# Order of queued ScalarE and VectorE work in an attention + two-layer MoE-style kernel

## The chip, the cores and the metric

The kernel runs on one core of one Trainium2 chip, as one launch. The metric is the device time of one execution in microseconds (us); the median of several runs is compared. One execution is also profiled, which gives the instruction trace of every engine: TensorE (PE, with its weight loads PEld), VectorE (DVE), ScalarE (ACT), GpSimd (POOL) and the DMA queues, of which SP issues most.

## What is computed

```
# q, k, v: [2, 8, 768, 64]; centroids: [8, 16, 64]; all float32
q_assign = argmax(normalize(q) @ normalize(centroids).T)      # 16 clusters a head
k_assign = argmax(normalize(k) @ normalize(centroids).T)
scores   = where(q_assign == k_assign, q @ k.T / 8, -1e9)
attn     = softmax(scores) @ v                                # -> x: [1536, 512]

# first layer, w_in [512, 2048], w_out [2048, 512] (float64 in memory)
x = softplus(x @ w_in) @ w_out
# second layer, w_gate, w_val [512, 1536], w_out2 [1536, 512] (float64 in memory)
out = (silu(x @ w_gate) * (x @ w_val)) @ w_out2               # [1536, 512]
```

## The kernel before, in words

Every float32 operand of the two layers is held as a high and a low part of TensorE's reduced format, and a product is three matmuls: high x high, high x low, low x high. `w_split` makes the two parts of a weight: a ScalarE cast (`whi`, line 151) and a subtraction (`wlo`, line 152), which by then is VectorE's. Ahead of it, weights stored in 64 bits are narrowed to 32 in steps: *first* (ScalarE, line 124, reads the freshly loaded `raw`), *second* (VectorE, lines 126 and 129), *third* (VectorE, lines 133 and 137; it also issues the next weight loads on the SP queue). `two_tasks` makes five tasks for two weights: first, second, third, split, split. `pair_tasks` makes nine: first, second, third, two tasks of sums, and four splits.

The order of work on each engine is the order in which the program issues it; nothing is reordered later. So every step below is also a place in a queue, and an instruction that waits holds all that stand behind it on its engine. Lists of tasks are handed to the places between products (`run(between[i])`), or popped from `todo` a few at a time (`pump2`).

The first layer has 16 blocks of 128 hidden columns. Blocks 0 to 5 are computed plainly. Blocks 6 to 15 go in pairs (p = 3 to 7), each by seven products instead of eight, with sums of quarters of x and of the weights: `block_a(p)` does three of them, `block_b(p)` four. A product (`prod`, line 1087) is 12 matmuls of 384 columns into a bank pair of PSUM. In `block_a` the first product goes to x, ScalarE copies it to `p1` (line 1110), the second goes to y, and the third adds onto x, so it has to wait for that copy. The softplus of the last quarter of the pair before (line 1155) reads the x of that pair. Casts and subtractions of the hidden values (`g_high`, line 919; `g_low`, line 923) give the second matrix its operands. What `block_b` returns is a list `late`, which `block_a` of the next pair runs in two parts.

`y_group(g)` is the second product of pair g, and stands between the blocks of later pairs: six pieces j, 12 matmuls of 512 columns each (line 1002), over bank pairs O, W, X, Y. Pieces 0 to 2 (near) are added by VectorE to an accumulator on the chip (line 1020). Pieces 3 to 5 (far) are copied by ScalarE to a side buffer (line 1023), two of which alternate by j, and a GpSimd DMA adds them to `far_acc` in DRAM (line 1028). After the last `y_group` three SP loads (line 1209) bring `far_acc` back. `y_last` is the second product of the last pair: VectorE adds each half piece to the accumulator (line 1040), ScalarE casts it to YH (line 1041), and GpSimd or VectorE makes YL (line 1047).

The second layer begins with `plain_unit(0)`: its matmuls (line 854) take six of the banks that `y_last` has just used, the third of them the first half of bank pair Y, used by piece 3 of `y_last`. `one_` and `two_` are the tasks of the gate and value weights of units 0 and 1. Units 2 to 11 are `s_unit(f)`: seven products each, with `more()` between them, which runs the tasks in `todo`, and `fill(n)`, output pieces (line 1328) whose copy to a side buffer is line 1341. `a_half` casts and subtracts the hidden values of a unit.

Of the kernel before, what the change touches and what calls it, by code (L numbers as in the profile page):

```python
# [15 lines left out]
AF = mybir.ActivationFunctionType  # L16
# [18 lines left out]
def _h(ap, n=2):  # L35

    return ap.rearrange("p (a n) -> p a n", a=n)
# [3 lines left out]
def kernel(  # L41
# [123 lines left out]
    NPL = 3  # L165
# [736 lines left out]
    def run(tasks):  # L902
        for task in tasks:
            task()
# [13 lines left out]
    def g_high(f, e, cols):  # L918
        nc.scalar.copy(g_t[f][0][:, cols], e[:, cols])  # L919

    def g_low(f, e, cols):
        gh, gl = (x[:, cols] for x in g_t[f])
        nc.vector.tensor_tensor(out=gl, in0=e[:, cols], in1=_r(gh), op=ALU.subtract)
# [87 lines left out]
    def y_group(g, tags, order, between, bk0=None):  # L1011
        near = accs[0].rearrange("p a n -> p (a n)")
        for i, j in enumerate(order):
            bk = y_piece(g, j, tags[i], None if i else bk0)
            if j < 3:
                a = _h(near[:, 1024 * j:1024 * j + 1024])
                if g == 0:
                    nc.scalar.copy(a, bk)
                else:
                    nc.vector.tensor_tensor(out=a, in0=bk, in1=a, op=ALU.add)  # L1020
            else:
                st = _h(side[j % 2][:, 0:1024])
                nc.scalar.copy(st, bk)  # L1023
                a = _h(far_acc[:, 1024 * (j - 3):1024 * (j - 3) + 1024])
                if g == 0:
                    nc.sync.dma_start(out=a, in_=st)
                else:
                    nc.gpsimd.dma_start(out=a, in_=st, accum_op=ALU.add)  # L1028
            run(between[i])
# [71 lines left out]

    T0, T1 = slice(0, HT), slice(HT, NTOK)
    now = {}

    def block_a(p, between, late=()):
        g1 = S_t[("in", p), "1"]
        x = px("OX"[p % 2], "x")[:, :, 0:HT // 2]
        prod(x, g1, 0, qx(0, 0), True)
        p1 = p1_p.tile([128, 2, HT // 2], F32, tag="p1", name="p1")
        nc.scalar.copy(p1, x)  # L1110
        run(late[:1])
        y = px("Y", "y")[:, :, 0:HT // 2]
        prod(y, g1, 2, qx(1, 0), True)
        ev = tp.tile([128, NTOK], F32, tag="e", name="ev")
        nc.vector.tensor_tensor(out=_h(ev[:, T0]), in0=y, in1=p1, op=ALU.add)
        nc.scalar.activation(out=ev[:, T0], in_=ev[:, T0], func=AF.Softplus)
        run(late[1:])
        run(between[0])
        g3 = S_t[("in", p), "3"]
        prod(x, g3, 2, tqx(2))  # L1120
        eg = tp.tile([128, NTOK], F32, tag="e", name="eg")
        nc.scalar.copy(_h(eg[:, T0]), x)
        run(between[1])
        now[p] = g3, x, ev, eg

    def block_b(p, between):
        g3, x, ev, eg = now.pop(p)
        g2, g4 = (S_t[("in", p), n] for n in "24")
        fg, fv = 2 * p, 2 * p + 1

        def soft(src, e, cols, f):
            nc.scalar.activation(out=e, in_=src, func=AF.Softplus)

        w = px("W", "w")[:, :, 0:HT // 2]
        prod(w, g2, 0, tqx(3), True)
        nc.scalar.copy(_h(eg[:, T1]), w)
        g_home(fv)
        g_high(fv, ev, T0)
        g_low(fv, ev, T0)
        run(between[0])  # L1140
        prod(x, g3, 0, tqx(1))
        nc.vector.tensor_tensor(out=_h(eg[:, T1]), in0=x, in1=_h(eg[:, T1]), op=ALU.add)
        nc.scalar.activation(out=eg[:, T1], in_=eg[:, T1], func=AF.Softplus)
        g_home(fg)
        g_high(fg, eg, T1)
        run(between[1])
        prod(w, g4, 0, tqx(4))
        nc.vector.tensor_tensor(out=_h(eg[:, T0]), in0=w, in1=_h(eg[:, T0]), op=ALU.add)
        g_low(fg, eg, T1)
        nc.scalar.activation(out=eg[:, T0], in_=eg[:, T0], func=AF.Softplus)  # L1150
        g_high(fg, eg, T0)
        run(between[2])
        prod(x, g2, 2, qx(1, 1))
        g_low(fg, eg, T0)
        nc.scalar.activation(out=_h(ev[:, T1]), in_=x, func=AF.Softplus)
        run(between[3])
        return [lambda: g_high(fv, ev, T1), lambda: g_low(fv, ev, T1)]

    def three(*tags):
        tiles = [px(tag, "bank") for tag in tags]  # L1160
# [28 lines left out]
    pair, outs = in_pair_tasks(NPL + 1), out_tasks(NPL)  # L1189
    block_a(NPL, (tx3[2:3], tx3[3:]), [soft5])  # L1190
    y_group(2, "OWYOWY", MIX, (pair[0:1], pair[1:2], pair[2:3], pair[3:5], pair[5:7] + outs[0:1], outs[1:2] + pair[7:8]))
    late = block_b(NPL, ([], outs[2:3], outs[3:4], [])) + outs[4:5] + pair[8:9]
    for p in range(NPL + 1, NPAIRS - 1):
        pair, outs = in_pair_tasks(p + 1), out_tasks(p)
        block_a(p, (pair[0:1], pair[1:2]), late)
        y_group(p - 1, ("OX"[p % 2 - 1] + "WY") * 2, MIX, (pair[2:3], pair[3:5], pair[5:7], [pair[7], outs[0]], outs[1:2], outs[2:3]))
        late = block_b(p, (outs[3:4], outs[4:5], [], [])) + pair[8:9]
    outs = out_tasks(NPAIRS - 1)
    one_, two_ = (two_tasks([("gate", f), ("val", f)], "ac") for f in range(2))
    block_a(NPAIRS - 1, (outs[0:1], outs[1:2]), late)  # L1200
    run(block_b(NPAIRS - 1, ([], outs[2:3], outs[3:4], outs[4:5] + one_[0:1])))
    nc.scalar.activation(out=p1_p.tile([128, 1], F32, tag="x3", name="early"), in_=id32[:, 0:1], func=AF.Silu)
    y_group(NPAIRS - 2, "OYWXOY", (3, 4, 5, 0, 1, 2), (
        one_[1:2], one_[2:3], one_[3:4], one_[4:5] + two_[0:1], two_[1:2], two_[2:3]
    ))
    accs.append(mp.tile([128, 2, NTOK], F32, tag="t4", name="acc"))
    back = accs[1].rearrange("p a n -> p (a n)")
# [12 lines left out]

    YH = keep.tile([128, KD, NTOK], F32R, tag="xh", name="YH")
    YL = keep.tile([128, KD, NTOK], F32R, tag="xl", name="YL")
    y_last(NPAIRS - 1, "WXOYWX", ([], two_[3:4], two_[4:5], [functools.partial(t_sum, 0)], [], []))


    outv = out.rearrange("(b p t) d -> b p t d", b=B, t=NT)
# [19 lines left out]
    def pump2(steps):  # L1246

        for _ in range(-(-len(todo) // steps)):
            todo.popleft()()
# [94 lines left out]
        else:  # L1344
            nc.gpsimd.dma_start(out=out_of(n), in_=st, accum_op=ALU.add)  # L1345

    def s_unit(f):
        g1, g2, g3, g4 = (S_t[f, n] for n in "1234")
        last = f == NF2 - 1

        def quarter(k, t):
            return lambda part, kk: (YH, YL)[part][:, 2 * k + kk, HT * t:HT * t + HT]

        def tq(n):
            return lambda part, kk: T_t[n][part][:, HT * kk:HT * kk + HT]

        def fill(n):
            if f < 2 or last:
                return
            g, h = divmod(f - 2, 2)  # L1360
            o_out(g, 3 * h + n)

        left = [9]

        def more():
            pump2(left[0])
            left[0] -= 1

        t1, t2 = 0, 1
        sg_all = tp.tile([128, NTOK], F32, tag="e", name="sg")  # L1370
        sg = sg_all.rearrange("p (t c n) -> p t c n", t=2, c=2)
        x = px("X", "x")[:, :, 0:HT // 2]
        prod(x, g1, 0, quarter(0, 0), True)
        p1 = p1_p.tile([128, 2, HT // 2], F32, tag="p1", name="p1")
        nc.scalar.copy(p1, x)
        more()
        w = px("W", "w")[:, :, 0:HT // 2]
        prod(w, g2, 0, tq(3), True)
        nc.scalar.copy(sg[:, t2], w)
        more()  # L1380
        prod(x, g3, 2, tq(2))
        nc.scalar.copy(sg[:, t1], x)
        more()
        prod(w, g4, 0, tq(4))
        nc.vector.tensor_tensor(out=sg[:, t1], in0=w, in1=sg[:, t1], op=ALU.add)
        nc.scalar.activation(out=sg[:, t1], in_=sg[:, t1], func=AF.Silu)
        more()
        fill(0)
        more()
        prod(x, g3, 0, tq(1))  # L1390
        nc.vector.tensor_tensor(out=sg[:, t2], in0=x, in1=sg[:, t2], op=ALU.add)
        nc.scalar.activation(out=sg[:, t2], in_=sg[:, t2], func=AF.Silu)
        more()
        y = px("Y", "y")[:, :, 0:HT // 2]
        prod(y, g1, 2, quarter(1, 0), True)
        nc.vector.tensor_tensor(out=p1, in0=y, in1=p1, op=ALU.add)
        a_t[f] = pieces_of(f)
        nc.vector.tensor_tensor(out=sg[:, t1], in0=p1, in1=sg[:, t1], op=ALU.mult)
        more()
        fill(1)  # L1400
        more()
        prod(x, g2, 2, quarter(1, 1))
        nc.vector.tensor_tensor(out=sg[:, t2], in0=x, in1=sg[:, t2], op=ALU.mult)
        more()
        fill(2)
        a_half(f, sg_all, 0)
        a_half(f, sg_all, 1)
# [2 lines left out]
    rest = plain_unit(0)  # L1410
    todo.extend(rest)
    todo.extend(pair_tasks(NPLAIN, ("gate", NPLAIN), ("val", NPLAIN), "4321"))
    todo.extend(two_tasks([("out2", f) for f in range(NPLAIN)], "bb"))
    rest = plain_unit(1)
    while todo:
        todo.popleft()()
    todo.extend(rest)
    for f in range(NPLAIN, NF2):
        if f + 1 < NF2:
            todo.extend(pair_tasks(f + 1, ("gate", f + 1), ("val", f + 1), "4321"))  # L1420
        todo.extend(split_tasks(last_of(f)))
        s_unit(f)
    assert not todo

    G = NF2 // 2 - 2
# [51 lines left out]
```

## Time and profile before

| | |
|---|---|
| median of 3 runs | 804.28 us (803.09 to 804.67) |
| the profiled execution | 803.32 us |
| its span, first to last instruction | 801.5 us |
| mean granted TensorE clock | 0.992 of full speed |
| TensorE busy | 784.1 us, 98% |
| VectorE busy | 631.9 us, 79% |
| ScalarE busy | 495.1 us, 62% |
| GpSimd busy | 180.4 us, 23% |
| bytes moved by DMA | 104.17 MB, mean 130 GB/s |

A busy share of TensorE is no measure of its speed: matmuls are pipelined and their ends are modelled, so what counts is how far apart they start. The other engines' shares are those of instructions that really ran. Times in the views are counted from the first instruction.

### The profile page before, as it was taken

What the parts mean: (1) busy time and instruction counts of PE and PEld (TensorE: products, weight loads), DVE (VectorE), ACT (ScalarE), POOL (GpSimd) and SP (SyncE); (2) the same over time, 40 slices, a digit from 0 to 9 for tenths busy, and PEclk for the clock granted to TensorE, in tenths of its full rate; (3) what the DMA queues carried; (4) which work ended last, traced back from release to release, by engine and by line L of the source; (5) the groups of instructions that cost most, each with busy time, mean ns of one, the idle gap of its engine ahead of it and who ended that gap; (6) DMA issues with size and microseconds to landing.
All of it is one profiled execution on the core that took longest, in us unless ns stands there. A gap on an engine that the chain in (4) does not pass through costs nothing.

```text
span 801.5 us, 12250 instructions
## 1 busy us (share of the span) xinstructions
PE 784.1 (98%) x4545; PEld 712.5 (89%) x4545; DVE 631.9 (79%) x1012; ACT 495.1 (62%) x895; POOL 180.4 (23%) x178
## 2 busy tenths in 40 slices
PE   8999999999999999999999999899999999999997
PEld 7898899999998888889889898688899999999996
DVE  5988978989898888888677765899777777777763
ACT  5888889889897474546456365355654555555520
POOL 5635655556432000100100101400000101011100
PEclk8999999999999999999999999999999999999999
DMA  7875865765512322734835626403445676767554
GB/s 185 222 176 128 195 159 130 182 150 141 132 31 51 105 105 79 184 75 110 183 79 106 127 69 159 145 0 106 158 158 106 134 155 136 154 120 145 85 178 158
DMA packets 72796, 104.17 MB, mean 130 GB/s; under 512 B 29760, under 2 KB 52384, under 8 KB 72736
## 3 DMA queue, kind: packets, MB, share of 16 engines
q1 hardware_dynamic: 65552, 82.54, 35.5%
q0 software_dynamic: 5616, 20.45, 16.7%
q8 instruction: 36, 0.59, 0.3%
q10 hardware_dynamic: 1568, 0.39, 0.2%
q14 instruction: 24, 0.20, 0.1%
HBM read 52.99 MB, written 28.36 MB: 101 GB/s over the span
## 4 chain that ended last, share of the span: by engine, by line
PE 79%; DVE 9%; ACT 6%; DMA 3%; issue 2%; POOL 0%; ACTq 0%; DVEq 0%; SPq 0%; POOLq 0%
PE ob L1002 12%; PE x L1087 12%; PE ob L1328 11%; PE bank L854 8%; PE ops L596 8%; PE tps L579 7%; PE sps L547 7%; PE w L1087 6%; PE y L1087 3%; DMA raw<-in_moe_w_val_dram 2%; PE mps L421 2%; PE sims L458 1%; DVE wlo L152 1%; DVE m L133 1%; ACT gh L919 1%
## 5 line engine op out<-in xcount | busy, mean ns | idle before, releaser
L586 DVE TENSOR_TENSOR tl<-tps,th 128x384 fp32r<-128x384 f32 x192 | 98.8, 551 | 14.7 <-ACT th L585 14.4
L555 DVE TENSOR_REDUCE nm<-sps 128x1 f32<-128x768 f32 x96 | 91.3, 952 | 13.6 <-PE sps L547 10.3
L585 ACT CAST th<-tps 128x384 fp32r<-128x384 f32 x192 | 84.9, 492 | 16.8 <-PE tps L579 13.9
L579 PE MATMUL tps<-id,p 128*128 128x128 f32 x576 | 93.4, 279 | 1.7 <-DVE tl L586 1.7
L563 ACT ACTIVATE p<-sps,nm 128x768 f32<-128x768 f32 x96 | 88.2, 919 | 1.6 <-DVE nm L555 1.5
L547 PE MATMUL sps<-KT,QT 128*128 128x384 f32 x384 | 83.3, 338 | 1.3 <-ACT p L563 1.3
L579 PEld LDWEIGHTS tps<-id,p 128*128 128x128 f32 x576 | 75.0, 150 | 9.0 <-DVE tl L586 5.1
L596 PE MATMUL ops<-th,VV 128*128 128x256 f32 x288 | 80.0, 307 | 0.0
L596 PE MATMUL ops<-tl,VV 128*128 128x256 f32 x288 | 72.6, 282 | 0.0
L152 DVE TENSOR_TENSOR wlo<-m,whi 128x512 fp32r<-128x512 f32 (+1 forms) x66 | 41.6, 640 | 39.1 <-ACT whi L151 38.7
L1345 POOL DMA_DIRECT2D out_dram<-side x21 | 18.1, 864 | 219.2 <-ACT side L1341 219.2
L1028 POOL DMA_DIRECT2D far_acc<-side x18 | 15.7, 872 | 225.9 <-ACT side L1023 225.9
L151 ACT CAST whi<-m 128x512 fp32r<-128x512 f32 (+1 forms) x62 | 34.3, 565 | 50.2 <-DVE m L137 50.2
L547 PEld LDWEIGHTS sps<-KT,QT 128*128 128x128 f32 x384 | 63.4, 189 | 1.9 <-ACT p L563 1.7
L1328 PE MATMUL ob<-whi,aa 128*128 128x512 f32 x168 | 56.8, 392 | 0.0
L596 PEld LDWEIGHTS ops<-tl,VV 128*128 128x128 f32 x288 | 54.7, 190 | 0.1
L596 PEld LDWEIGHTS ops<-th,VV 128*128 128x128 f32 x288 | 54.4, 189 | 0.2
L1002 PE MATMUL ob<-gh,whi 128*128 128x512 f32 x168 | 51.8, 389 | 0.0
L1002 PE MATMUL ob<-gh,wlo 128*128 128x512 f32 x168 | 51.8, 389 | 0.0
L1002 PE MATMUL ob<-gl,whi 128*128 128x512 f32 x168 | 51.8, 389 | 0.0
L124 ACT ACTIVATE m<-raw 128x512 f32<-128x512 f32 x68 | 43.5, 669 | 9.8 <-DVE wlo L152 6.7
L1023 ACT COPY side<-ob 128x1024 f32<-128x1024 f32 x21 | 21.2, 1015 | 42.9 <-PE ob L1002 37.8
(254 smaller groups left out, 1995.7 us busy)
## 6 DMA issues: line engine op xcount, KB each, us to landing
raw<-in_moe_w_out_dram SPq DMA_DIRECT2D x28, 512.0 KB, 4.2
out_dram<-side POOLq DMA_DIRECT2D x21, 512.0 KB, 5.6
far_acc<-side POOLq DMA_DIRECT2D x18, 512.0 KB, 6.2
raw<-in_moe_w_in_dram SPq DMA_DIRECT2D x16, 512.0 KB, 6.1
raw<-in_moe_w_gate_dram SPq DMA_DIRECT2D x12, 512.0 KB, 3.6
raw<-in_moe_w_val_dram SPq DMA_DIRECT2D x12, 512.0 KB, 4.2
QT<-hi SPq DMA_DIRECT2D x30, 192.0 KB, 3.1
KT<-hi SPq DMA_DIRECT2D x14, 384.0 KB, 5.7
```

The lines of the kernel that those rows point to most:

```text
L152: low_on[0].tensor_tensor(out=lo, in0=x, in1=_r(hi), op=ALU.subtract)
L547: nc.tensor.matmul(ps[:, c, 0:384], lhsT=Q[:, a, 128 * j:128 * j + 128], rhs=K[:, a, 384 * c:384 * c + 384], start=(a == 0), stop=(a == 1),)
L555: nc.vector.tensor_reduce(out=nm, in_=ps[:, :, 0:384], axis=AX.XY, op=ALU.max, negate=True)
L563: nc.scalar.activation(out=_h(p), in_=s_t.pop(i)[:, :, 0:384], func=AF.Exp, bias=nm_t.pop(i), accum_out=sm_t[pr][:, j:j + 1],)
L579: nc.tensor.transpose(ps[:, 128 * j:128 * j + 128], p[:, 128 * kb:128 * kb + 128], id32)
L585: nc.scalar.copy(th, pv)
L586: nc.vector.tensor_tensor(out=tl, in0=pv, in1=_r(th), op=ALU.subtract)
L596: nc.tensor.matmul(o[:, 0:CW], lhsT=VV_t[pr][:, hh, kb].rearrange("p a d -> p (a d)"), rhs=t[:, kb, :], start=(kb == 0 and lohi == 0), sto ...
L854: nc.tensor.matmul(banks[c], lhsT=wt[:, kk, :], rhs=xt[:, kk, 512 * c:512 * c + 512], start=(kk == 0 and wt is hi and xt is xh), stop=(kk ...
L1002: nc.tensor.matmul(bk[:, t, :], lhsT=wt[:, 0, 128 * d:128 * d + 128], rhs=gt[:, 512 * c:512 * c + 512], start=(ff == 0 and n == 0), stop=( ...
L1087: nc.tensor.matmul(dst[:, c, :], lhsT=wt[:, at + kk, :], rhs=x(part, kk)[:, HT // 2 * c:HT // 2 * c + HT // 2], start=(first and kk == 0 a ...
L1328: nc.tensor.matmul(bk[:, t, :], lhsT=lhs[:, ts_], rhs=rhs[:, 0, :], start=(ff == 0 and i == 0), stop=(ff == 1 and i == 2),)
```

## The change

Four things move, and nothing is computed differently.

1. In `block_b` the last cast, softplus and subtraction of the gate half are not issued in place but returned in `late`, now five entries: cast of the gate half, last softplus, cast of the value half, and the two subtractions. `block_a` runs four entries of the list right after the copy of line 1110, and the rest after its softplus. The last split of the next pair's weights (`pair[8:9]`) moves from `late` to the fourth place of `block_b`.
2. In the last `y_group` the pieces run near and far in turns, 3, 1, 4, 2, 5, 0 instead of 3, 4, 5, 0, 1, 2.
3. The weight splits of unit 0 move one place earlier, together with the third step; the tasks of unit 1 move one place earlier each, and its two splits go from `y_last` to the last place of that `y_group`.
4. Of the tasks for the second layer's first two output weights, the third step now follows the evictions of unit 1, and the two splits stand in the second `more()` of `s_unit(2)`; unit 1's `a_half` casts all stand in its first `more()`.

```diff
+    LATE = 4
     def block_a(p, between, late=()):
...
         nc.scalar.copy(p1, x)
-        run(late[:1])
+        run(late[:LATE])
...
         nc.scalar.activation(out=ev[:, T0], in_=ev[:, T0], func=AF.Softplus)
-        run(late[1:])
+        run(late[LATE:])
...
         nc.scalar.activation(out=eg[:, T0], in_=eg[:, T0], func=AF.Softplus)
-        g_high(fg, eg, T0)
         run(between[2])
         prod(x, g2, 2, qx(1, 1))
-        g_low(fg, eg, T0)
-        nc.scalar.activation(out=_h(ev[:, T1]), in_=x, func=AF.Softplus)
         run(between[3])
-        return [lambda: g_high(fv, ev, T1), lambda: g_low(fv, ev, T1)]
+        def last_soft():
+            nc.scalar.activation(out=_h(ev[:, T1]), in_=x, func=AF.Softplus)
+        return [
+            lambda: g_high(fg, eg, T0), last_soft, lambda: g_high(fv, ev, T1),
+            lambda: g_low(fg, eg, T0), lambda: g_low(fv, ev, T1),
+        ]
...
-    late = block_b(NPL, ([], outs[2:3], outs[3:4], [])) + outs[4:5] + pair[8:9]
+    late = block_b(NPL, ([], outs[2:3], outs[3:4], pair[8:9])) + outs[4:5]
...
-        late = block_b(p, (outs[3:4], outs[4:5], [], [])) + pair[8:9]
+        late = block_b(p, (outs[3:4], outs[4:5], [], pair[8:9]))
...
-    y_group(NPAIRS - 2, "OYWXOY", (3, 4, 5, 0, 1, 2), (
-        one_[1:2], one_[2:3], one_[3:4], one_[4:5] + two_[0:1], two_[1:2], two_[2:3]
+    y_group(NPAIRS - 2, "OYWXOY", MIX[1:] + MIX[:1], (
+        one_[1:2], one_[2:5], two_[0:1], two_[1:2], two_[2:3], two_[3:5]
     ))
...
-    y_last(NPAIRS - 1, "WXOYWX", ([], two_[3:4], two_[4:5], [functools.partial(t_sum, 0)], [], []))
+    y_last(NPAIRS - 1, "WXOYWX", ([], [], [], [functools.partial(t_sum, 0)], [], []))
...
-    def s_unit(f):
+    def s_unit(f, lead):
...
         def more():
-            pump2(left[0])
+            if lead:
+                run(lead.pop(0))
+            else:
+                pump2(left[0])
             left[0] -= 1
...
-    todo.extend(two_tasks([("out2", f) for f in range(NPLAIN)], "bb"))
+    outs = two_tasks([("out2", f) for f in range(NPLAIN)], "bb")
+    todo.extend(outs[:2])
     rest = plain_unit(1)
     while todo:
         todo.popleft()()
-    todo.extend(rest)
+    run(outs[2:3])
     for f in range(NPLAIN, NF2):
...
-        s_unit(f)
+        s_unit(f, [rest, outs[3:]] if f == NPLAIN else [])
```

## Rows read from the trace of the kernel before

**Rows 1.** The page, busy time of each engine: TensorE's line.

```profile
PE 784.1 (98%) x4545; PEld 712.5 (89%) x4545; DVE 631.9 (79%) x1012; ACT 495.1 (62%) x895; POOL 180.4 (23%) x178
```

**Rows 2.** Waits of TensorE, 300 us to the end: total, times, longest.

```profile
PE bank L854 <- ACT YH L1041: 3.0, 1, 3.0
PE x L1087 <- ACT p L1110: 1.4, 3, 0.5
PE x L1087 <- ACT p L1375: 0.6, 1, 0.6
```

**Rows 3.** Timeline of TensorE into pair 7: start, us, what.

```profile
467.67 0.51 PE L1087 MATMUL y<-XH,wlo 128*128 128x384 f32 x2
468.66 0.98 PE L1087 MATMUL x<-Tx,whi 128*128 128x384 f32 x4 [0.49 <-ACT p L1110]
...
471.04 0.62 PE L1087 MATMUL w<-XH,whi 128*128 128x384 f32 x2
...
473.29 0.85 PE L1087 MATMUL x<-Tx,whi 128*128 128x384 f32 x4
```

**Rows 4.** Timeline of ScalarE and VectorE in the same stretch.

```profile
465.50 0.85 ACT L1150 ACTIVATE eg<-eg 128x768 f32<-128x768 f32 x1 [1.63 <-DVE eg L1148]
...
467.82 0.79 ACT L1110 COPY p<-x 128x768 f32<-128x768 f32 x1
...
468.64 0.96 DVE L1115 TENSOR_TENSOR ev<-y,p 128x768 f32<-128x768 f32 x1 [0.44 <-ACT p L1110]
...
469.63 0.85 ACT L1116 ACTIVATE ev<-ev 128x768 f32<-128x768 f32 x1 [0.29 <-DVE ev L1115]
...
470.38 0.60 ACT L151 CAST whi<-side 128x512 fp32r<-128x512 f32 x1
...
470.89 1.24 ACT L124 ACTIVATE m<-raw 128x512 f32<-128x512 f32 x2
...
472.03 0.80 ACT L1122 COPY eg<-x 128x768 f32<-128x768 f32 x1
```

**Rows 5.** The chain that ended last, 330 to 560 us: start, us, what.

```profile
370.80 2.08 PE y L1087 x12
...
372.90 2.36 PE x L1087 x12
375.26 16.36 PE ob L1002 x72
...
490.49 9.23 DMA raw<-in_moe_w_val_dram
```

**Rows 6.** Timeline of all engines at the turn of the layers.

```profile
504.86 1.28 DVE L1040 TENSOR_TENSOR acc<-ob,acc 128x512 f32<-128x512 f32 x2
...
512.22 0.64 PE L854 MATMUL bank<-YH,whi 128*128 128x512 f32 x2
...
513.10 1.39 DVE L152 TENSOR_TENSOR wlo<-m,whi 128x512 fp32r<-128x512 f32 x1 [1.21 <-ACT whi L151]
514.42 1.28 DVE L1040 TENSOR_TENSOR acc<-ob,acc 128x512 f32<-128x512 f32 x2
...
515.84 0.47 PE L854 MATMUL bank<-YH,whi 128*128 128x512 f32 x1 [2.99 <-ACT YH L1041]
```

**Rows 7.** Windows: busy time (count) by engine, clock, DMA share, GB/s.

```profile
516.00:520.00 4.00, 4.00 (x11) 3.12 (x11) 3.93 (x5) 1.57 (x4) 3.39 (x2) 0.57 0.01 4
```

**Rows 8.** DMA queues, 491 to 495 us (q0 GpSimd, q1 SP): packets, MB, share.

```profile
q0 software_dynamic: 171, 0.63, 99.8%
q1 hardware_dynamic: 12, 0.01, 1.5%
```

**Rows 9.** Tile `raw`, 470 to 520 us: time of its loads to landing.

```profile
DMA to landing us min/median/max: 4.4/8.4/12.5
```

**Rows 10.** Tile `acc`, 480 to 530 us: reload issues (ns, first and last start), landing.

```profile
L1209 SPq DMA_DIRECT2D acc<-far_acc x3: 382/423/567, 505.4 to 506.3; - x3
...
DMA to landing us min/median/max: 6.9/7.2/7.6
```

## The prediction, as written before the changed kernel was run

> **What bounds the kernel now.** I read the page first: TensorE is busy nearly the whole span [rows 1], so only the places where it stands still can pay. The view of waits, TensorE alone, from the first layer's weights to the end, names three such places [rows 2]: one wait of 3.0 us for a bank in the second layer's first unit (line 854), three of about 0.5 us for the copy of line 1110, and one of 0.6 us for line 1375. The timeline of each place then says how much later than due the next matmul began. The profile models a matmul's end, so starts are compared.
>
> At a pair boundary [rows 3], twelve matmuls of one product take 2.08 us [rows 5], so two take 0.35. The last two of y began at 467.67 and x was due at 468.02; it began at 468.66. Its first four then took 0.98 instead of 0.85. The boundary costs 0.64 + 0.13 = 0.77 us. The reader is to see why in ScalarE's queue [rows 4]: line 1110 empties the bank that x adds to, and starts at 467.82 because line 919 and the softplus of line 1155 stand ahead of it in the queue, though its input had been complete since y began, at 468.02 - 2.08 = 465.9.
>
> At the turn of the layers [rows 6], the first unit's third matmul was due at 512.22 + 2 x 0.23 = 512.68 and began at 515.84: 3.16 us. It wanted a bank that VectorE empties with the two additions (line 1040) at 514.42. Ahead of these stands a weight subtraction (line 152) at 513.10, which waited for its cast and took 1.39 us, where two additions of that width take 1.28. (A piece's matmuls follow each other by 16.36 / 72 = 0.227 [rows 5].) After the wait the granted clock was 0.57 on average over 4 us [rows 7] (1.2 GHz is 0.50, 2.4 GHz is 1.00): 4 x 0.43 = 1.7 us more.
>
> **The change, part by part.**
>
> *Bank copy first.* At the boundaries into pairs 5 and 6 ScalarE's order becomes: softplus 1150, the cast of the pair's last split (from the fourth place of block_b), copy 1110, then cast, softplus, cast. From [rows 4], which are those into pair 7 but stand for all: 1150 at 465.50, the cast 0.75 later (as 470.38 follows 469.63), the copy 0.51 later (as 470.89 follows 470.38) at 466.76, done at 467.55. That is before 468.02, so both waits go: 2 x 0.77 = 1.54. Into pair 4 there is little to win: y 2.08, x 2.36 [rows 5], so 0.28.
>
> Into pair 7, block_b follows at once, and ScalarE's work is only permuted. Copy 466.76, cast of the gate half about 467.5 to 468.3 (0.8, as line 1110 over as many elements), VectorE's subtraction of that half now ahead of line 1115, each 0.96 as that line's row has it, so softplus 1116 at about 470.2 (469.63 before); then two line-124 conversions and copy 1122 at 470.2 + 0.75 + 1.14 = 472.1, done 472.9. The x product of block_b reads behind that copy: 472.95 instead of 473.29 [rows 3], less a start of 0.13: 0.2 us, although the waits ahead of it vanish: 0.77, and 0.28 where w, due at 468.66 + 0.13 + 2.08 = 470.87, began at 471.04 and started as slowly (0.11). Queued behind the delayed 1116 are those conversions and VectorE's work on them; nothing on TensorE wants them for a product or more. The first term is 0.28 + 1.54 + 0.2 = **2.0 us**; ends 0 (the wait comes back at another bank, below) and 2.9 (pair 7 loses nothing).
>
> What this costs: softplus 1155 now frees its bank after the copy, about 467.55 + 0.7 + 0.85 = 469.1. The next y_group's first piece wants that bank at 468.02 + 2.08 = 470.1. Cover 1.0 us, hence nothing; a later copy costs its excess once per pair.
>
> *Splits out of y_last.* The two casts and two subtractions for unit 1 leave the eviction chain. A piece has 12 matmuls, 16.36 / 6 = 2.73 us [rows 5]; counted back from 512.22, pieces 0 to 5 of y_last are due at 495.9, 498.6, 501.3, 504.0, 506.8 and 509.5. Piece 3 ends at 506.8, so its additions need no longer wait for a split. The term is 3.16 + 1.7 = **4.9 us** if the bank is free by 512.7.
>
> *Where they go.* They now stand ahead of y_last, which makes VectorE's first eviction later, counted from the landing L of the last value weights. Before, L was 490.49 + 9.23 = 499.7 [rows 5] and the first eviction 504.86 [rows 6], 5.1 later. Two subtractions of 0.7 make it L + 6.5, and the bank for piece 4 free at L + 7.8. It is due at 506.8: no wait while L is under 499.0, beyond that one us for each. The evictions then run on: ten of 0.65 us to the bank in question, at L + 13 at the latest, in time while L is under 499.7.
>
> Why L should move: near and far pieces in turns put one accumulating transfer, not two, ahead of it. From 491 to 495, with the load issued at 490.49, the SP queue moved 12 packets, 0.01 MB of its 512 KB, while GpSimd's queue held the engines for 99.8% of the time [rows 8] with the transfers of two far pieces. One near addition now precedes the third step, so the load is issued about 1.3 later, near 491.8 (two additions, [rows 6]); with the shortest landing of 4.4 [rows 9], L is 496.2 as an estimate, with the longest of 12.5 it is 504.3. I take 496.2, since the second far transfer then follows the load.
>
> A rule speaks against this. The Trainium skill (DMA: Bandwidth & Descriptors, Queues, rings and completion order) says that each DMA engine takes turns between its queues, packet by packet. By that rule a queue's order would not bring L forward, and the sum would hold the second rival's 0.7 us wait. The rows disagree: 12 packets of this queue beside 171 of the other are no turns.
>
> *The same step's other queues.* The third step of unit 1 issues two weight loads on SP, now a piece earlier; the three reloads of the far accumulator stand behind them on SP and move too: from 505.4 [rows 10], 5.7 after L and with a near addition between, to about L + 4.4 = 500.6. They took 6.9 to 7.6 us to land, so near 508. Far piece 4's copy stands behind the casts of unit 0, which wait for VectorE: the second cast ends near 493.0, the copy with at most 1.3 at 494.3; its bank is due at 495.9, cover 1.6. Far piece 5's copy stands behind the conversion that waits for L: L + 0.6 + 1.3 = 498.1, its bank is due at 501.3, cover 3.2. Each costs its excess if the cover goes.
>
> *The second layer's start.* The out-weight casts move behind the evictions of unit 1. Four operations of 0.7 us lie between the second more() and fill(0), beside two products (4.2 us): nothing, or their excess. The wait of 0.6 at line 1375 (about 0.9 with the slow start) is VectorE's backlog. The same VectorE work stays ahead of it, in another order, so it may vanish (+0.9) or grow as much (-0.6, one row's size). No row settles it; evictions that come before splits favour a gain, and I take **0.3**.
>
> Sum: 2.0 + 4.9 + 0.3 = 7.2 us. The profiled execution took 803.32 us (its span 801.5 and 1.8 around it), which makes 796.1; the median of the runs is 0.96 above it, so against 804.28 the forecast is **797.1**. From the likeliest case's ends: with all of pair 7 and of line 1375 (0.9 + 0.6 more) gives 795.6; with line 1375 grown and only 1.1 at the boundaries, 798.9.
>
> **The rivals.**
>
> *The reload holds the bank.* The additions of piece 3 are the first that read the reloaded half. If the reload waits for the last far piece, now fifth instead of third, it is issued no earlier than before. Before, it landed about 505.4 + 7.2 = 512.6; then 1.28 for two additions, and the matmul at 514.0: 1.3 of the 4.9 stays. 798.4. For it: only the wait behind the split hid this. Against it: each reload reads one far piece, and the first two are early.
>
> *L stays.* At 499.7 piece 4 waits 0.7: 797.8. For it: two queues share the engines at any order. Against it, [rows 8]. (The Trainium skill's rule above would give this one.)
>
> *The boundaries give nothing.* The softplus behind the copy holds the next bank by what the copy won: 799.1. Against it, the cover of 1.0.
>
> *No change.* L at its slow end, 504.3: piece 4 waits 5.3, and a wait that long brings the clock down again (1.7), so 7.2 - 7.0 = 0.2: 804.1.
>
> *Slower.* The same conversion of line 124, now ahead of far piece 5's copy and of every eviction, waits past 504.5. From there 7.8 after L, and the clock, cost more than 7.2. At L = 508 it is 9.0 + 1.7 - 7.2 = 3.5 over: 807.8. For it: a load of this weight took 12.5 [rows 9]. Against it: that one stood behind two far pieces.
>
> **How the numbers follow.** A measurement of this kernel can tell about 0.2% (1.6 us) from no change. Chances: likeliest 0.56, reload 0.14, L stays 0.08, boundaries nothing 0.07, no change 0.08, slower 0.07. Faster takes the first four, less a hundredth: 0.84; same 0.09; slower 0.07. The range leaves out the last two and the edge above 798.9 that no rival gives: 795.0 to 800.8, the low end half a us under the best case, the high one at the boundaries' rival with line 1375 grown and L late.
>
> **What would show it.** After: line 1110 ends before y does at pairs 5 and 6, and no wait for it is left; x of block_b still follows line 1122 at pair 7. No line 152 between the evictions of y_last; the first unit's third matmul follows the second at once, and the clock stays at 1.00. Line 124 for the last value weights starts near 496. If the bank still waits with the evictions idle before a reload, the reload is the cause; if y_last's piece 4 waits, L is. A new wait at y_group's first piece would undo the boundaries.

## Result, and the profile after

The changed kernel takes 797.03 us (median of 4 runs, 796.30 to 798.76), the kernel before, timed beside it, 804.47 us (4 runs, 803.09 to 804.76). The ratio is 0.9914 with a 95% interval of 0.9894 to 0.9934: 7.4 us faster. The profiled execution took 796.3 us, its span is 794.5 us (before: 801.5). The forecast was 797.1.

The page, the span and each engine's busy time:

```profile
span 794.5 us, 12255 instructions
PE 780.4 (98%) x4545; PEld 710.4 (89%) x4545; DVE 632.7 (80%) x1012; ACT 495.6 (62%) x895; POOL 179.9 (23%) x178
```

The work is that of [rows 1]; TensorE's busy time is 3.7 us less for the same 4545 matmuls. The view of waits, TensorE alone, 300 us to the end (total, times, longest):

```profile
PE x L1087 <- ACT eg L1123: 0.7, 1, 0.7
PE x L1087 <- ACT p L1383: 0.2, 1, 0.2
```

Against [rows 2] the wait of 3.0 us at line 854 and the three for the copy of line 1110 (now 1111) are gone. Line 1375 (now 1383) keeps 0.2 of 0.6. One wait is new: the x product of pair 7's block_b stands behind the copy of line 1123 (before, 1122).

**Where the 7.0 us of span came from.** Both programs issue the same 4545 matmuls in the same order, so the start of each can be set against the start of its counterpart (below: by starts). The changed kernel is 0.54 us *late* behind 225 us, in a stage that the change doesn't touch. From there it gains: into pair 4 0.29; into pair 5 0.79; into pair 6 0.75; around pair 7 0.09 net; at the first unit's third matmul 3.17, and in the slow clock behind it 1.70; in the second layer's start 0.77. Together 7.56, less 0.54 is 7.02, and the spans differ by 801.5 - 794.5 = 7.0. The stage ahead drifts in either direction (the changed kernel was 1.77 us ahead at 18 us, 0.72 ahead at 212 and 0.53 behind at 225), so differences of spans alone can't resolve half a microsecond here; starts on either side of one place can.

TensorE's timeline at the boundary into pair 6 (start, us, what):

```profile
435.23 0.51 PE L1087 MATMUL y<-XH,wlo 128*128 128x384 f32 x2
435.58 0.85 PE L1087 MATMUL x<-Tx,whi 128*128 128x384 f32 x4
```

The last two matmuls of y and the first of x now are 0.35 apart, as two matmuls take, and x starts at full pace (0.85 for four). At the boundary into pair 7 it is the same, but what was won is lost again in block_b:

```profile
466.38 0.51 PE L1087 MATMUL y<-XH,wlo 128*128 128x384 f32 x2
466.73 0.85 PE L1087 MATMUL x<-Tx,whi 128*128 128x384 f32 x4
...
468.81 0.51 PE L1087 MATMUL w<-XH,whi 128*128 128x384 f32 x2
...
470.54 0.51 PE L1087 MATMUL w<-XH,wlo 128*128 128x384 f32 x2
471.79 0.98 PE L1087 MATMUL x<-Tx,whi 128*128 128x384 f32 x4 [0.73 <-ACT eg L1123]
```

The last line was due at 470.54 + 0.35 = 470.89 and began 0.90 late, then took 0.98 instead of 0.85: 1.0 us. ScalarE's queue over the same stretch shows why:

```profile
464.96 0.60 ACT L151 CAST whi<-side 128x512 fp32r<-128x512 f32 x1
465.47 0.79 ACT L1111 COPY p<-x 128x768 f32<-128x768 f32 x1
...
469.09 0.85 ACT L1117 ACTIVATE ev<-ev 128x768 f32<-128x768 f32 x1 [0.51 <-DVE ev L1116]
469.84 1.20 ACT L124 ACTIVATE m<-raw 128x512 f32<-128x512 f32 x2
470.95 0.78 ACT L1123 COPY eg<-x 128x768 f32<-128x768 f32 x1
```

The copy of line 1111 ends at 466.26, before y does. In [rows 4] it began only 0.2 us before x was due. The copy of line 1123 still stands behind a softplus and two conversions.

At the turn of the layers, the timelines of GpSimd, of SP and of ScalarE, in the changed kernel:

```profile
486.86 0.86 POOL L1028 DMA_DIRECT2D far_acc<-side  x1 [30.46 <-ACT side L1023]
492.13 1.07 POOL L1028 DMA_DIRECT2D far_acc<-side  x1 [4.41 <-ACT side L1023]
```

```profile
489.73 0.37 SPq L101 DMA_DIRECT2D raw<-in_moe_w_val_dram  x1
```

```profile
489.70 1.22 ACT L151 CAST whi<-m 128x512 fp32r<-128x512 f32 x2 [3.14 <-DVE m L137]
490.83 1.01 ACT L1023 COPY side<-ob 128x1024 f32<-128x1024 f32 x1
...
494.81 0.66 ACT L124 ACTIVATE m<-raw 128x512 f32<-128x512 f32 x1 [2.40 <-DMA raw<-in_moe_w_val_dram]
```

The last value weights are issued at 489.73 and used at 494.81, 5.1 us later, where they took 9.23 before [rows 5]. Only one accumulating transfer is ahead of them; the second is issued at 492.13, because its copy (490.83) stands on ScalarE behind unit 0's two casts, which waited 3.14 us for VectorE. The view of the DMA queues from 490 to 495 (packets, MB, share) shows SP's queue moving 1032 packets, this load and the next, where it moved 12 in [rows 8]:

```profile
q1 hardware_dynamic: 1032, 1.03, 59.7%
q0 software_dynamic: 117, 0.41, 45.8%
```

The first unit's matmuls and the window over them (busy time and count by engine, clock, DMA share, GB/s):

```profile
510.84 0.84 PE L854 MATMUL bank<-YH,whi 128*128 128x512 f32 x3
511.52 0.84 PE L854 MATMUL bank<-YL,whi 128*128 128x512 f32 x3
```

```profile
510.00:515.00 5.00, 5.00 (x24) 4.14 (x23) 4.91 (x5) 1.82 (x3) 2.05 (x3) 1.00 0.00 0
```

Three follow one another without a gap, where [rows 6] has two and then 2.99 us of waiting, and the granted clock is 1.00 (2.4 GHz) instead of 0.57 [rows 7].

### The profile page after: what moved, and what is told of

The parts are those of the page before. It is cut to its first block, busy times and chain, and to the rows that moved or that the text cites. A ratio compares the mean times of both kernels' runs of the same rounds, so it can differ in the third digit from the quotient of the medians.

```text
span 794.5 us, 12255 instructions
## 1 busy us (share of the span) xinstructions
PE 780.4 (98%) x4545; PEld 710.4 (89%) x4545; DVE 632.7 (80%) x1012; ACT 495.6 (62%) x895; POOL 179.9 (23%) x178
## 4 chain that ended last, share of the span: by engine, by line
PE 87%; DVE 5%; ACT 3%; DMA 3%; issue 1%; POOL 0%; SPq 0%; ACTq 0%; DVEq 0%; POOLq 0%
PE ob L1002 16%; PE x L1087 14%; PE ob L1333 11%; PE bank L854 10%; PE ops L596 7%; PE w L1087 7%; PE tps L579 7%; PE sps L547 7%; PE y L1087 3%; PE mps L421 2%; PE sims L458 1%; DMA rd<-R 1%; DMA R<-rd 1%; DVE tl L586 1%; DVE nm L555 1%
## 5 line engine op out<-in xcount | busy, mean ns | idle before, releaser
L137 DVE SCALAR_TENSOR_TENSOR m<-raw,m 128x512 int32<-128x512 int32 x68 | 44.6, 685 | 0.6
```

Source lines behind the costliest of these rows:

```text
L137: nc.vector.scalar_tensor_tensor(out=m, in0=lo, scalar=29, in1=m, op0=ALU.logical_shift_right, op1=ALU.bitwise_or)
```

## Experiments

Each is named by what it changes; times are medians of its runs and of the kernel before on the same chip, with the ratio's 95% interval.

**Pair blocks alone** (before, with only the new order in block_a and block_b):

```
-        run(late[:1])
+        run(late[:LATE])
...
+        return [
+            lambda: g_high(fg, eg, T0), last_soft, lambda: g_high(fv, ev, T1),
+            lambda: g_low(fg, eg, T0), lambda: g_low(fv, ev, T1),
+        ]
```

> The kernel before with part 1 of the change alone (bank copy ahead of the casts in the blocks). Parts add: about 1.9 us under before (802.5 against 804.4): matmul starts gain 0.28, 0.76 and 0.76 into pairs 4, 5 and 6 and about 0.1 into pair 7, where x then waits about 1 us for line 1123; the 3.1 us wait at the turn of the layers and its slow clock stay. Rival, the turn absorbs it: the value weights land no earlier, so the wait at line 854 grows by what the blocks won, and the time is within 0.5 us of before. Rival, the boundaries give nothing: a new wait at the first y_group piece, 804.4.

Measured: 801.77 us against 804.07, ratio 0.9975 [0.9958, 0.9992]. The boundaries gain by starts what they gain in the full change, and pair 7 shows the same new wait for line 1123. The wait at line 854 stayed, 3.07 us by starts, but this time the clock did not fall behind it. TensorE's timeline, and the window behind the wait:

```profile
513.34 0.47 PE L854 MATMUL bank<-YH,whi 128*128 128x512 f32 x1 [2.92 <-ACT YH L1041]
```

```profile
514.00:518.00 4.00, 4.00 (x20) 3.27 (x18) 3.91 (x5) 1.72 (x3) 3.83 (x2) 1.00 0.01 4
```

About 1.1 us of new waits came in unit 2, by starts. The first term stands by itself. That the clock falls behind such a wait does not hold in this execution.

**Splits and turns alone** (before, with only the new places of unit 0's casts and unit 1's splits and the new order of pieces):

```
-    y_group(NPAIRS - 2, "OYWXOY", (3, 4, 5, 0, 1, 2), (
-        one_[1:2], one_[2:3], one_[3:4], one_[4:5] + two_[0:1], two_[1:2], two_[2:3]
+    y_group(NPAIRS - 2, "OYWXOY", MIX[1:] + MIX[:1], (
+        one_[1:2], one_[2:5], two_[0:1], two_[1:2], two_[2:3], two_[3:5]
...
-    y_last(NPAIRS - 1, "WXOYWX", ([], two_[3:4], two_[4:5], [functools.partial(t_sum, 0)], [], []))
+    y_last(NPAIRS - 1, "WXOYWX", ([], [], [], [functools.partial(t_sum, 0)], [], []))
```

> The kernel before with parts 2 and 3 alone (last y_group near and far in turns, splits of units 0 and 1 in their new places, none in y_last). Parts add: the wait of 3.1 us at line 854 and the slow clock of 1.7 both go, 4.8 us under before (799.6), with the block waits as before. Rival, the reload holds the bank: 1.3 us of the wait stays and the clock holds, 3.5 under. Rival, the gain needs part 1 too: less than 2 us under.

Measured: 799.50 against 804.07, 0.9945 [0.9927, 0.9963]. By starts the turn gains 4.87 us, the wait and the slow clock both; the block waits are as before. The second term stands by itself too, but 0.47 us of it is lost again in unit 2, where the product w now waits for ScalarE (the last row). Its waits of TensorE:

```profile
PE x L1087 <- ACT p L1110: 1.5, 3, 0.5
PE x L1087 <- ACT p L1375: 0.6, 1, 0.6
PE w L1087 <- ACT sg L1379: 0.2, 1, 0.2
```

**Far pieces first** (the changed kernel with the old order of pieces):

```
-    y_group(NPAIRS - 2, "OYWXOY", MIX[1:] + MIX[:1], (
+    y_group(NPAIRS - 2, "OYWXOY", (3, 4, 5, 0, 1, 2), (
```

> The changed kernel with the far pieces first again (3, 4, 5, 0, 1, 2), everything else as changed. Theory, the load of the last value weights runs after the accumulating transfers that are ahead of it: line 124 for it starts 3 us later than the changed kernel's 494.8, near 498; with one more near addition behind it, piece 4 of y_last waits 1 to 2 us; about 1.5 us over the changed kernel, 798.5. Rival, the queues take turns packet by packet, so order doesn't matter: it starts within 0.5 us of 494.8 and the time is that of the changed kernel, 797.0.

Measured: 799.92 against 804.07, 0.9952 [0.9932, 0.9973], 2.9 us above the changed kernel's median and 2.0 by starts. GpSimd's queue, and the conversion on ScalarE:

```profile
487.09 1.78 POOL L1028 DMA_DIRECT2D far_acc<-side  x2 [30.44 <-ACT side L1023]
```

```profile
496.93 0.66 ACT L124 ACTIVATE m<-raw 128x512 f32<-128x512 f32 x1 [2.76 <-DMA raw<-in_moe_w_val_dram]
```

Two accumulating transfers go out back to back, and the load issued at 488.83 is used 8.1 us later instead of 5.1. TensorE then loses 0.47 us at y_last's fourth piece, whose bank waits for the last near addition (line 1020), and 1.55 in the third column of the first unit. The transfers ahead delay the load.

**Output weights alone** (before, with only the second layer's new places for out2's splits):

```
-    todo.extend(two_tasks([("out2", f) for f in range(NPLAIN)], "bb"))
+    outs = two_tasks([("out2", f) for f in range(NPLAIN)], "bb")
+    todo.extend(outs[:2])
...
-        s_unit(f)
+        s_unit(f, [rest, outs[3:]] if f == NPLAIN else [])
```

> The kernel before with part 4 alone (third step and splits of the first two output weights, a_half of unit 1). The wait at the copy into unit 3 (line 1375 of before, 0.8 us late plus a slow start) falls to about 0.4 and the 0.25 at the third output piece goes: 0.8 us under before, 803.6, as the matmul starts of the changed kernel show it. Rival, that gain came from the earlier turn of the layers and not from part 4: 0.0 and the wait stays.

Measured: 802.84 against 804.07, 0.9990 [0.9976, 1.0005]: the runs don't resolve it. By starts, 0.25 of wait in unit 2 is gone and the one at line 1375 falls from 0.8 to 0.34: 0.75 us with the slow starts. The wait at line 854, 2.8 us here, is followed by the low clock, as the window over the 4 us behind it has it:

```profile
517.00:521.00 4.00, 4.00 (x12) 3.17 (x11) 3.91 (x6) 1.57 (x4) 3.60 (x2) 0.57 0.01 4
```

**Splits put back** (the changed kernel with unit 1's two splits in y_last again; all else as changed):

```
-        one_[1:2], one_[2:5], two_[0:1], two_[1:2], two_[2:3], two_[3:5]
+        one_[1:2], one_[2:5], two_[0:1], two_[1:2], two_[2:3], []
...
-    y_last(NPAIRS - 1, "WXOYWX", ([], [], [], [functools.partial(t_sum, 0)], [], []))
+    y_last(NPAIRS - 1, "WXOYWX", ([], two_[3:4], two_[4:5], [functools.partial(t_sum, 0)], [], []))
```

> The changed kernel with the two splits of unit 1 put back into places 2 and 3 of y_last, everything else as changed. Theory as predicted, the place of the splits is the cause: the subtraction stands again between the evictions, the third matmul of the first unit waits about 3 us and the clock falls, 4.8 us over the changed kernel, 801.8. Rival, the early landing is the cause: the evictions run early enough that the split fits between them, the bank is free near 511.3 and due at 511.3, so the wait is 0 to 0.5 us with no fall of the clock, 797.0 to 797.5.

Measured: 795.16 against 804.33, 0.9900 [0.9876, 0.9925]. Nothing of the 4.9 us is lost. VectorE, then TensorE:

```profile
505.90 1.41 DVE L152 TENSOR_TENSOR wlo<-m,whi 128x512 fp32r<-128x512 f32 x1 [1.21 <-ACT whi L151]
507.24 1.27 DVE L1040 TENSOR_TENSOR acc<-ob,acc 128x512 f32<-128x512 f32 x2
```

```profile
509.24 0.84 PE L854 MATMUL bank<-YH,whi 128*128 128x512 f32 x3
```

The subtraction stands ahead of the two additions, waits 1.21 us for its cast and takes 1.41, as in [rows 6], and yet the bank is free at 508.5, in time, because the whole chain of evictions runs earlier: the load was used at 492.42, some 4 us after its issue at 488.40. What the prediction named as the cause is not needed for the gain.

**Order of pieces alone** (before, with nothing but the turns) and **splits out alone** (before, with nothing but the splits moved to the end of y_group):

```
-    y_group(NPAIRS - 2, "OYWXOY", (3, 4, 5, 0, 1, 2), (
+    y_group(NPAIRS - 2, "OYWXOY", MIX[1:] + MIX[:1], (
```

> The kernel before with the pieces of the last y_group near and far in turns and nothing else: all weight tasks in their old places, two splits in y_last. Theory, the early landing alone is enough: with one accumulating transfer ahead, the last value weights take 4 to 5 us from issue to line 124 instead of 9, the evictions start 2 us earlier, and the wait of 3.1 us at line 854 goes or stays under 0.5 although the splits stand in the chain; 4 us under before, 800.2. Rival, as predicted, the splits in the chain are the cause: at least 2.5 us of the wait stays, 804.

Measured: 803.80 against 803.73, 0.9995 [0.9980, 1.0010]. The turns by themselves do not bring the load forward. GpSimd, then ScalarE:

```profile
490.25 1.77 POOL L1028 DMA_DIRECT2D far_acc<-side  x2 [31.05 <-ACT side L1023]
```

```profile
501.40 0.66 ACT L124 ACTIVATE m<-raw 128x512 f32<-128x512 f32 x1 [6.26 <-DMA raw<-in_moe_w_val_dram]
```

Both far transfers go out before the load's issue at 493.12, since unit 0's casts still stand behind the second copy on ScalarE, and the load takes 8.3 us. The wait at line 854 is 2.94 us, with no fall of the clock behind it; what that saves is lost again in unit 2, 1.1 us by starts.

```
-        one_[1:2], one_[2:3], one_[3:4], one_[4:5] + two_[0:1], two_[1:2], two_[2:3]
+        one_[1:2], one_[2:3], one_[3:4], one_[4:5] + two_[0:1], two_[1:2], two_[2:5]
...
-    y_last(NPAIRS - 1, "WXOYWX", ([], two_[3:4], two_[4:5], [functools.partial(t_sum, 0)], [], []))
+    y_last(NPAIRS - 1, "WXOYWX", ([], [], [], [functools.partial(t_sum, 0)], [], []))
```

> The kernel before with the two splits of unit 1 moved from y_last to the end of the last y_group and nothing else: far pieces first, all else in its old place. Theory as predicted, with the splits out the bank is free in time: no wait at the third matmul. The landing stays late (8 to 9 us after its issue), so the first eviction is later than before, y_last's piece 4 waits about 1 us and the unit's third column of matmuls waits about 2 us for low parts that GpSimd and VectorE make, as in the kernel with far pieces first; 1 to 2 us under before, 802.5. Rival, only the landing counts: the wait of 3 us stays, 804.

Measured: 802.89 against 803.73, 0.9996 [0.9977, 1.0015]. The load is issued at 489.49 and used at 498.11, 8.6 us later. The third matmul is on time, but the late chain shows at other places: 0.5 us at y_last's fifth piece, and 1.85 us on TensorE in the third column, which begins:

```profile
517.32 0.50 PE L854 MATMUL bank<-YH,whi 128*128 128x512 f32 x1 [0.84 <-ACT YH L1041]
```

By starts 2.4 us are lost at the turn, against 3.4 with the pair blocks alone, where the splits stand in y_last, the load is as late and the clock does not fall either. Another 1.05 us goes in unit 2. So taking the splits out is worth about 1 us where the load is late, and nothing measurable where it is early.

**Conversions behind the copy** (the changed kernel; a task of pair 7's output weights, the two line-124 conversions, moved from the place ahead of line 1123 to the next one):

```
-    block_a(NPAIRS - 1, (outs[0:1], outs[1:2]), late)
+    block_a(NPAIRS - 1, ([], outs[0:2]), late)
```

> The changed kernel with the two conversions (line 124) that stand ahead of the bank copy 1123 at pair 7 put behind it. Theory, that copy is what x of pair 7 waits for, and the queue ahead of it is the reason: the wait of about 1.0 us (0.9 late, 0.1 slow start) goes, 796.0. Rival, the wait comes back at line 1143 or later in the block, because ScalarE and VectorE have the same work: less than 0.3 us gained, 796.8.

Measured: 794.70 against 804.33, 0.9890 [0.9866, 0.9914]. The wait for line 1123 is gone from the view of waits, which keeps 0.2 us at line 1383 alone. By starts 0.9 us is won there, 0.2 of it is lost at the next x product, and 0.7 stays. ScalarE, then TensorE:

```profile
469.40 0.80 ACT L1123 COPY eg<-x 128x768 f32<-128x768 f32 x1
470.10 1.22 ACT L124 ACTIVATE m<-raw 128x512 f32<-128x512 f32 x2
```

```profile
470.29 0.95 PE L1087 MATMUL x<-Tx,whi 128*128 128x384 f32 x4
```

This is the best version by its trace. Its interval overlaps the changed kernel's, so that it beats it rests on the starts.

**The last wait, into unit 3.** In the changed kernel the copy of line 1383 stands on ScalarE behind a weight cast that waits for VectorE:

```profile
567.26 0.62 ACT L151 CAST whi<-m 128x512 fp32r<-128x512 f32 x1 [4.29 <-DVE m L137]
568.69 1.57 ACT L1248 CAST aa<-sg 128x768 fp32r<-128x768 f32 x2
570.16 0.80 ACT L1383 COPY p<-x 128x768 f32<-128x768 f32 x1
```

Three kernels tried to move that cast. First, issued after a_half in unit 2, alone and together with the conversions behind the copy:

```
-        more()
+        if f > NPLAIN:
+            more()
         fill(2)
...
         a_half(f, sg_all, 1)
+        if f == NPLAIN:
+            more()
```

> The changed kernel with the last weight task of unit 2 (third step and split of an output weight) issued behind that unit's casts instead of ahead of its last output piece. Theory, the cast that waits for VectorE holds the copies of ScalarE behind it and so the bank copy into unit 3: its wait of 0.44 us goes, 796.6. Rival, the bank copy waits for the unit's own casts: 797.0.

> The changed kernel with both moves of the two kernels before this one. If both waits go and nothing else takes their place, 1.4 us under the changed kernel, 795.6. If the block's wait comes back later, 796.5.

Measured: 799.17 against 804.33, 0.9937 [0.9914, 0.9959], and with both 798.61, 0.9934 [0.9914, 0.9954]. These intervals overlap the changed kernel's; by starts both are worse, by 2.0 us at this place and 1.6 more in the slow clock of the profiled executions. ScalarE, TensorE and the window behind them in the first of the two:

```profile
572.70 0.62 ACT L151 CAST whi<-m 128x512 fp32r<-128x512 f32 x1 [2.49 <-DVE m L137]
```

```profile
574.07 0.80 PE L1087 MATMUL x<-Th,whi 128*128 128x384 f32 x2 [2.19 <-ACT p L1383]
```

```profile
574.00:578.00 4.00, 3.93 (x14) 3.93 (x15) 3.36 (x8) 1.84 (x4) 0.00 (x0) 0.57 0.29 112
```

The cast is still ahead of the copy, and the VectorE work it waits for now comes after ScalarE's casts of line 1248: TensorE waits 2.35 us by starts, and the clock falls. That the cast holds the copy is right; the edit put it in a worse place.

Then unit 2's output-weight splits left to unit 3, with the conversions behind the copy:

```
-        todo.extend(split_tasks(last_of(f)))
+        if f > NPLAIN:
+            todo.extend(split_tasks((last_of(NPLAIN) if f == NPLAIN + 1 else []) + last_of(f)))
```

> The changed kernel with the conversions behind the bank copy at pair 7, and with the three tasks of unit 2's own output weight taken out of unit 2 and done in unit 3, ahead of unit 3's. If the cast that waits for VectorE was what held the bank copy into unit 3, that wait of 0.44 us goes, the one of 1.0 at pair 7 goes, and the time is 1.4 us under the changed kernel. Rival, unit 3 is now as full as unit 2 was and its own copy into unit 4 waits 0.4 us or more: 1.0 or less under.

Measured: 795.85 against 803.73, 0.9897 [0.9874, 0.9920]. The 0.44 us into unit 3 is gone and comes back larger into unit 4 (0.11 + 0.76 + 0.1), behind the same kind of cast, which waits 4.12 us for VectorE there. TensorE:

```profile
594.06 0.61 PE L1087 MATMUL x<-Th,whi 128*128 128x384 f32 x2 [0.60 <-ACT p L1383]
```

**The changed kernel again**, beside the last three on one chip:

> The changed kernel once more, on the same chip as the three others: 0.991 of before, matmul starts after 300 us as in its first profile (a wait of 1.0 us at pair 7 and of 0.4 us into unit 3, none at the turn of the layers).

Measured: 795.61 against 803.73, 0.9903 [0.9881, 0.9925]; the two waits are those of its first profile, 0.7 and 0.2, and there is none at the turn.

## Why the prediction was right, and where it was not

The time, and the size of two of the three terms, came out as forecast; of the second, the cause that the prediction put first was wrong, so that its size came out is in part luck.

- **Bank copy first: 2.0 predicted, 1.92 measured.** 0.29 into pair 4; 0.79 and 0.75 into pairs 5 and 6, where 0.77 each was taken; around pair 7 0.09 net where 0.2 was taken. The step "the x product of block_b reads behind that copy" held: the waits ahead vanish (0.79 at x, 0.31 at w) and line 1123 takes 1.01 back. The experiment with the conversions moved shows that it is they that hold it: 0.9 us returns, 0.7 of it for good. The cover of 1.0 for the softplus behind the copy was enough: no wait at y_group's first piece. The rival "the boundaries give nothing" falls.
- **The turn: 4.9 predicted, 4.87 measured, by another cause.** The step that failed is "Splits out of y_last": it says that the additions of piece 3 are in time because no split stands ahead of them. With the splits put back nothing was lost; with only the splits out, 2.4 of 3.4 us stayed. What brings the gain is the step "Why L should move". It forecast the last value weights at 496.2, in the times of the kernel before; they were used at 494.81, when TensorE was 1.37 us ahead, which is the same place. Two errors cancelled in that: the load went out 0.7 earlier than forecast and took 5.1 us where the shortest landing of 4.4 was taken. (The longest, 12.5 in [rows 9], which the prediction gives to "a load of this weight", is that of the gate weights issued behind it; the value weights took 9.23.) Before, the split was the last in a chain that was late anyhow, so the row in [rows 6] showed true things (it waited, and took 1.39) and not the cause.
- **Why L moved: half told.** The prediction credits the turns: one accumulating transfer ahead of the load, not two. That the number of transfers ahead decides is shown: 8.1 to 8.6 us from issue to use with two ahead (far pieces first, turns alone, splits out alone; 9.23 before), 4.0 to 5.1 with one. But the turns alone still had two ahead. Unit 0's casts must also come a place earlier, ahead of the second far copy on ScalarE: their wait for VectorE holds that transfer back, to 2.4 us after the load's issue. The prediction saw that queue ("Far piece 4's copy stands behind the casts of unit 0") and took it as a risk with a cover of 1.6; it is half of the mechanism. That these casts hold the copy is read from the traces; the edit that moved them also moved unit 1's tasks a place earlier, and no run has one without the other. The prediction's working against its own step, from turns between the queues, was wrong too. By the bytes per packet above and in [rows 8], a load of 512 KB is some 512 packets of 1 KB, and an accumulating transfer some 140 of 3.7 KB. So, as an estimate, the load would end after both transfers even if the queues took turns packet by packet, and sooner with one ahead; its times from issue to use do not tell turns from order.
- **The clock: 1.7 predicted, 1.70 measured**, and the size holds for this pair of executions only; that is luck. After waits of about the same length at line 854 it fell in two kernels (3.16 us before, 2.8 with the output weights alone) and did not in two (3.07 with the pair blocks alone, 2.94 with the turns alone). With no wait there, in the changed kernel and its variants, it never fell at that place.
- **Second layer's start: 0.3 predicted, 0.77 measured**, inside the bounds of +0.9 and -0.6. The term was mis-sized: most of the 0.9 came. The output weights alone gave 0.75 by starts. The prediction adds the terms, but this part does more beside an earlier turn. Without it, TensorE came to unit 2 early and waited there for ScalarE: 0.47 us with splits and turns alone, 1.05 to 1.1 with the pair blocks, the turns and the splits out alone. In the changed kernel and with the far pieces first, which have it, that wait is not there.
- **Rivals.** "The reload holds the bank" falls: three of the first unit's matmuls start together, with no wait at line 854. "L stays" falls as an outcome; the three kernels in which L did stay late (far pieces first, splits out alone, turns alone) lost 2.0 to 3.6 us at the turn; only the splits out alone lost part of it at the fifth piece, as that rival has it. "No change" and "slower" needed L at 504.3 or later; the latest seen was 501.40, with the turns alone. The time there was that of before, but not by the wait of 5.3 us at piece 4 that "no change" has: the waits at line 854 and in unit 2 stayed or came, and by starts 0.33 was lost at y_last's third piece, behind the late copy of far piece 5 that "slower" names.

By terms the sum is 7.56, 0.4 more than forecast, and the drift ahead of 225 us took 0.54 back. The nearness of 797.03 to 797.1 is in part that.

## What to carry to other kernels

To learn why a chain is late, put one part of the change back: an instruction that waits and stands last ahead of the stall need not be what made the chain late. In a queue that runs in order, an early cast that waits for another engine also holds whatever is behind it; that can help, when it keeps a large transfer from going ahead of one that is needed sooner, or hurt, when it holds a bank's copy. Compare kernels with the same instructions start by start at one place: it resolved 0.3 us here, where the runs could not resolve 1.

## What the runs showed of the hardware

- The SP queue's load of 512 KB took 4.0 to 5.1 us from issue to use beside one accumulating transfer issued ahead by GpSimd, and 8.1 to 9.3 beside two. The Trainium skill (DMA: Bandwidth & Descriptors, Queues, rings and completion order) has each engine take turns between its queues packet by packet. The counts show no even turns by the profile's packets: 12 beside 171 in [rows 8], and 38 beside 65 in the same trace from 494 to 496. The times from issue to use, as worked out above, decide nothing about it.
- VectorE operations with both inputs in SBUF took up to twice as long beside GpSimd's subtractions. GpSimd, then VectorE, in the changed kernel:

```profile
503.07 4.39 POOL L1047 TENSOR_TENSOR YL<-acc,YH 128x512 fp32r<-128x512 f32 x3 [5.54 <-ACT YH L1041]
507.64 2.99 POOL L1047 TENSOR_TENSOR YL<-acc,YH 128x512 fp32r<-128x512 f32 x2 [0.18 <-ACT YH L1041]
```

```profile
506.22 1.87 DVE L1040 TENSOR_TENSOR acc<-ob,acc 128x512 f32<-128x512 f32 x3
508.18 1.30 DVE L1047 TENSOR_TENSOR YL<-acc,YH 128x512 fp32r<-128x512 f32 x1
509.40 2.84 DVE L1219 TENSOR_TENSOR acc<-acc 128x1536 f32<-128x1536 f32 x1
512.17 1.87 DVE L1040 TENSOR_TENSOR acc<-ob,acc 128x512 f32<-128x512 f32 x3
...
516.71 0.69 DVE L1047 TENSOR_TENSOR YL<-acc,YH 128x512 fp32r<-128x512 f32 x1 [0.69 <-ACT YH L1041]
517.32 1.75 DVE L1219 TENSOR_TENSOR acc<-acc 128x1536 f32<-128x1536 f32 x1
```

  GpSimd subtracts until 510.63. In that time VectorE's subtraction of 512 columns takes 1.30 us and that of 1536 columns (line 1219) 2.84; once GpSimd has stopped (its last subtraction ends at 516.57), 0.69 and 1.75. The 1.09 us more of line 1219 is about what GpSimd still had to go when it began (510.63 - 509.40 = 1.23). The additions that read one input from a PSUM bank (ob) take 0.62 each either way: three at 506.22 beside GpSimd (until 507.46), three at 512.17 without it. The split at 1.39 in [rows 6] and at 1.41 with the splits put back is the same: each began while GpSimd still subtracted (until 513.94 and 506.77) and ended 0.55 us after it. The Trainium skill (SBUF — State Buffer, SBUF: two separate sides) says that VectorE, with two inputs in SBUF, and GpSimd share a pair of ports that one instruction holds alone until it is done; these rows agree.
- The granted clock fell to 0.57 over 4 us after waits of 2.35, 2.8 and 3.16 us and stayed at 1.00 after waits of 2.94 and 3.07: the length of a wait alone did not decide it.
- Two executions drift apart and together again ahead of 225 us, where no edit acts: from a lead of 1.77 us at 18 us to a lag of 0.53 at 225.
